# Attention outputs computed token-major and turned afterwards, some by DMA, with filler matmuls at the start and a new plan

## The chip, the cores and the metric

The kernel runs on one core of a Trainium2 chip. The metric is the device time of one execution in microseconds, the median of several executions; the kernel before takes 190.69 us (six runs, 190.32 to 191.94).

## The reference

Two stages follow each other. The first is a gated linear attention over 4 batches, 8 heads, 768 positions and 48 values per head: with f = sigmoid(f_logit) the state S of 48x48 is updated at each position t by

```python
state = f[:, :, t, :, None] * state + np.einsum('bhd,bhe->bhde', k[:, :, t], v[:, :, t])
y[:, :, t] = np.einsum('bhd,bhde->bhe', q[:, :, t], state)
```

The second stage takes y as x, 3072 tokens of 384 values, and computes

```python
h = x @ w_in
g = h * np.cos(h)
return (g @ w_out)
```

Everything comes in and goes out in float32 in DRAM.

## The kernel before, in words

**Tiles.** The 3072 tokens are 24 chunks of 128, six to a batch. Chunks 0 to 11 are worked on two at a time ("pairs" 0, 2, 4, 6, 8, 10, the list DUAL): a pair's tokens are loaded so that each partition holds two neighbouring tokens, an even and an odd one, and all the pair's tiles carry an index e for the two. Chunks 12 to 23 are worked on singly. Each chunk, or pair, goes through these steps, in the words that the code uses as names:

- `decay`: exp and ln of the gate on ScalarE (lines 482 and 494), a prefix sum over tokens on TensorE (`cum`, lines 505 to 517), and its exponentials `b` and `bi` on ScalarE (line 522).
- `attend2` for pairs, `attend` for single chunks. q and k are multiplied by b and bi (`qk`, lines 567 and 680). They are turned so that the head dimension lies on partitions: on TensorE against an identity (`tr`, lines 587 and 698) with a copy out of PSUM (`qkt`), or, for chunks 12 to 22 (TURN_QK), by one DMA transpose issued by SyncE (`tq`, line 689). Then come the scores q times k (`sc`, lines 600 and 711), their mask on VectorE (`am`, lines 606 and 714), k times v for the state (`ps`, lines 620 and 724), the state update (`st` on VectorE, `sz` mostly on GpSimd), and the output y.
- The output y is computed feature-major: features on partitions and tokens along the free axis. For that the 384 features are cut into twelve slices of 32, and each matmul loads 32 columns of v or of the state as weights and streams 128 tokens past them (line 653 for pairs, line 744 for single chunks). VectorE or ScalarE copies the result to the bfloat16 tile xT (`xe`).
- `moe` works on units of 128 or 256 tokens: `h` is x times w_in (line 768, groups of 12 matmuls for 256 tokens), `cos` on ScalarE (line 775), `g` the product on VectorE (line 778), `o` is g times w_out (line 790, groups of four matmuls), `ot` the copy out of PSUM, `st_o` the store. In a pair's chunk the rows of the output are the even and the odd tokens in two blocks, so the chunk is stored by two DMAs of 64 rows each, row by second row (line 799); a single chunk is stored by one (line 802).

The weights are loaded in eight slabs (`w00` to `w13`), each through a buffer of the gT pool, and cast to bfloat16 (line 430).

**What sets the order.** Nothing is scheduled by the hardware or by a compiler. `build` records operations with their possible engines and an estimated cost on each, and with priorities from the table PR; `Plan.run` places them one after the other on the engine that could take them first by these estimates, hands out buffers and PSUM banks, and emits all instructions in that order. PIN fixes the engine of single operations by their number. Each engine works its own list strictly in order. SyncE issues all loads, stores and DMA transposes from one list; a transfer there that waits for a buffer holds up all behind it.

Of the kernel before, what the change touches and what calls it, by code (L numbers as in the profile page):

```python
# [116 lines left out]
class Plan:  # L117
# [4 lines left out]
    FORM = 96.0  # L122
    TABLE = 1290.0
# [34 lines left out]
    def run(self):  # L158
        free = {"PE": 0.0, "ACT": 800.0, "DVE": 3500.0, "POOL": 4500.0, "SP": 750.0}
        table, lock, bus, hot, pe_end, form, sent = None, None, 0.0, 0.0, 0.0, "full", []  # L160
        left = {}
# [8 lines left out]
        while len(order) < n:  # L170
# [46 lines left out]
            o.cost = cost  # L217
            if e == "PE":
                hot *= math.exp((pe_end - s) / 2500.0)
                if hot < 0.5:  # L220
                    cost *= 1.9
                hot = 1.0 - (1.0 - hot) * math.exp(-cost / 2500.0)
                pe_end, form = s + cost, o.form[1]
            o.start = s
            free[e] = s + cost
            if o.dma is not None:
                bus = max(s + cost + 700.0, bus) + o.dma
                o.end = bus + 1250.0
# [19 lines left out]
        order.sort(key=lambda o: (o.start, o.seq))  # L248
        self.makespan = max(o.end for o in order)
# [3 lines left out]
def apart(tc, o, base):  # L253
# [13 lines left out]
    if banks and len(others) == len(banks):  # L267
        for b in banks:
# [8 lines left out]
HALVED = [0, 2]  # L277
TURN_QK = range(12, 23)
PR = {
    "at": [1.29, -46.96, -60.77, -65.31, -72.81, -88.9, -62.2, -78.56, -65.41, -84.16, -49.49, 6.81, 12.89,  # L280
          14.83, 48.99, 87.93, 101.11, 142.54, 101.56, 112.3, 125.58, 54.78, 57.75, 54.86],
    "dec": [47.91, 7.43, -56.35, -90.55, -146.08, -64.43],
    "f": [-34.92, 30.83, -12.01, 57.34, 6.81, 46.82, 6.06, 8.26, 16.01, 51.17, 25.08, -28.88, 70.17, 25.27,
          33.52, 29.11, 45.05, 53.82, 30, 41.02, 75.42, 105.25, 101.8, 47.02],
    "h": [18.15, -30.97, -41.55, -0.98, 22.93, -34.89, 0.62, 10.73, 30.17, 30.71, 68.39, 4.86, 95.08],
    "k": [-26.25, -35.58, -7.84, -14.12, 9.23, 20.62, 9.36, 29.64, 15.73, -3.08, 14.9, 28.23, 13.74, 17.17,
          50.2, 52.92, 39.09, 29.41, 58.65, 34.81, 116.3, 77.26, 139.17, 143.04],
    "o": [24.63, -19.31, 41.7, 78.77, 63.07, 110.4, 28.5, 147.24, 133.25, 171.17, 181.78, 182.53, 223.04],
    "tq": [40.18, 24.86, 49.05, 16.89, -14.63, -13.53, -72.99, 30.71, 100.53, 84.21, 40.41, 92.28, 63.29,
          8.72, -34.92, -31.89, -4.13, 9.55, 29.5, 39.68, 64.12, 95.56, 100.49, 121.09],  # L290
    "v": [-13.48, 17.98, -0.36, -1.26, 5.93, -16.14, 10.21, 31.08, 11.8, 9.11, 19.3, 20.54, 41.94, 22.2,
          47.4, 31.46, 38.38, 19.76, 32.92, 47.16, 53.68, 101.87, 117.21, 44.48],
    "w_in": [-6.83, -2.34, 0.21, 1.62],
    "w_out": [4.81, 3.28, 2.34, 8.4],
    "wc": [-90.87, -90.11, -69.83, -52.76, -136.89, -232, -120.5, -196.66],
    "gate": [None, 8, 6, 1, 19, 12],
}
PIN = {1: "POOL", 3: "ACT", 5: "ACT", 9: "DVE", 11: "POOL", 13: "DVE", 34: "POOL", 37: "POOL", 39: "ACT", 43:
       "ACT", 54: "DVE", 55: "DVE", 82: "DVE", 102: "POOL", 103: "POOL", 104: "DVE", 105: "POOL", 107: "DVE",
       111: "DVE", 124: "ACT", 164: "DVE", 165: "POOL", 167: "ACT", 169: "ACT", 182: "DVE", 204: "DVE", 210:  # L300
       "ACT", 222: "DVE", 228: "DVE", 243: "ACT", 244: "ACT", 283: "POOL", 284: "POOL", 286: "DVE", 293: "ACT",
       306: "ACT", 333: "DVE", 346: "POOL", 347: "POOL", 348: "POOL", 349: "POOL", 364: "ACT", 386: "ACT", 415:
       "ACT", 430: "ACT", 451: "DVE", 457: "DVE", 472: "POOL", 481: "ACT", 487: "ACT", 496: "DVE", 517: "DVE",
       523: "ACT", 547: "DVE", 558: "ACT", 579: "DVE", 585: "DVE", 600: "POOL", 608: "DVE", 623: "ACT", 644:
       "DVE", 665: "POOL", 674: "DVE", 680: "ACT", 689: "DVE", 731: "ACT", 740: "DVE", 746: "ACT", 752: "DVE",
       773: "DVE", 779: "ACT"}


def build(nc, cpool, ppool, q, k, v, f_logit, moe_w_in, moe_w_out, out):
# [13 lines left out]

    ident = tl([128, 128], BF16, "ident")
# [56 lines left out]
    stS = slots("st", 2, [128, NP, 2, D], F32)  # L381
    xS = slots("xT", 5, [128, KM, 256])
# [12 lines left out]
    P.banks = base  # L395
    HB = lambda a, d=D: a.rearrange("p (h d) -> p h d", d=d)
# [36 lines left out]
    def load(t, src, b, c, n, prio, nm, flat=lambda a: a):  # L433

        if n not in DUAL:
            P.op(nm + str(n), {"SP": 430.0}, lambda e: nc.sync.dma_start(
                out=HB(t.ap), in_=src[b, :, c * C:(c + 1) * C, :].rearrange("h p d -> p h d")),
                writes=[t], prio=prio, dma=1050.0)
# [116 lines left out]

    E = lambda e: nc.vector if e == "DVE" else nc.gpsimd

    def attend2(b, c, n, ld, bt, bi, prio):
# [6 lines left out]
        for i in range(2):  # L565
# [8 lines left out]
            reads=[vf], writes=[vb], prio=prio)  # L574
        twin = lambda j, p, e: qkv()[:, j, e, 2 * p:2 * p + 2, :].rearrange("p h d -> p (h d)")
        vv = lambda: vb.ap.rearrange("p (e h d) -> p e h d", e=2, d=64)[:, :, :, 0:D]
        rows = [slice(64 * x, 64 * x + 64) for x in range(2)]
        qkts, ams = [], []
        for i in range(2):
            pt, qkt, sc, am = Val(p1S), Val(qktS), Val(scS), Val(amS)  # L580

            def tr(e, i=i, pt=pt):
# [5 lines left out]
            P.op("tr", {"PE": mm(128, 8)}, tr, reads=[parts[0][i], parts[1][i]], writes=[pt], prio=prio)  # L588
            P.op("qkt", {"DVE": dve(1024, 0.52), "ACT": act(1024)}, lambda e, pt=pt, qkt=qkt: cp(
                e, qkt.ap, pt.ap.bitcast(BF16).rearrange("p (a n) -> p a n", n=C)),  # L590
                reads=[pt], writes=[qkt], prio=prio)

            def scores(e, qkt=qkt, sc=sc):
                o = sc.ap.rearrange("p (r a n) -> p r a n", r=2, n=C)
# [302 lines left out]
```

## Time and profile before

One execution was profiled. Its own time is 190.32 us; the span from its first to its last instruction is 188.5 us, so 1.8 us lie outside the span.

| | |
|---|---|
| median of six runs | 190.69 us |
| profiled execution | 190.32 us |
| span | 188.5 us |
| TensorE busy | 178.5 us, 2512 matmuls |
| VectorE busy | 130.5 us |
| ScalarE busy | 125.8 us |
| GpSimd busy | 68.1 us |
| moved by DMA | 33.14 MB, most of it in packets under 512 B |

The busy time of TensorE counts each matmul from its start to its end, and consecutive matmuls overlap, so it tells that the engine is seldom empty, not how fast it goes. How long a group of matmuls holds the engine is read from the start of the group to the start of the next one, as the chain of waits and the timeline show them.

### The profile page before, as it was taken

How to read it: one execution, taken by the hardware profiler on the slowest of the kernel's cores; microseconds unless marked ns; L12 is line 12 of the kernel's file. 1: busy time of each engine (PE TensorE's matmuls, PEld its weight loads, DVE VectorE, ACT ScalarE, POOL GpSimd, SP SyncE). 2: the span in 40 equal slices, each digit the busy share in tenths (PEclk: the TensorE clock that was granted, in tenths of full speed). 3: DMA queues.
4: the chain of work that ended last, by engine and by line, in shares of the span. 5: the costliest groups of instructions: out<-in, count | busy, mean ns of one | idle time of the engine just before them, and what ended most of it. 6: DMA issues, size and time to landing. Idle time of an engine off the chain costs nothing.

```text
span 188.5 us, 5879 instructions
## 1 busy us (share of the span) xinstructions
PE 178.5 (95%) x2512; PEld 132.8 (70%) x2512; DVE 130.5 (69%) x161; ACT 125.8 (67%) x152; POOL 68.1 (36%) x102
## 2 busy tenths in 40 slices
PE   0889999999999999999999999999999999999993
PEld 0567878666678866678976668856686776788663
DVE  5368798849796939965794285999289399366610
ACT  5771878987377897888899658899662460266411
POOL 8417253019411128793174694026842202000000
PEclk9999999999999999999999999999999999999999
DMA  5999999999998969998999999899710901102022
GB/s 151 271 301 352 381 370 255 287 252 260 251 229 199 228 128 183 226 177 159 188 219 162 187 183 180 169 182 183 170 45 0 122 36 39 48 3 83 0 83 83
DMA packets 94121, 33.14 MB, mean 176 GB/s; under 512 B 87312, under 2 KB 92560, under 8 KB 94096
## 3 DMA queue, kind: packets, MB, share of 16 engines
q1 hardware_dynamic: 94096, 32.78, 76.1%
q8 instruction: 19, 0.31, 0.7%
q14 instruction: 6, 0.05, 0.1%
HBM read 25.17 MB, written 4.72 MB: 159 GB/s over the span
## 4 chain that ended last, share of the span: by engine, by line
PE 82%; DVE 5%; SPq 3%; DMA 2%; ACT 2%; issue 2%; POOL 1%; POOLq 0%; DVEq 0%; ACTq 0%
PE ps L768 33%; PE ps L790 30%; PE ps L653 5%; SPq L444 3%; PE ps L744 3%; DVE qk L567 3%; DMA ld<-in_q_dram 2%; PE ps L711 2%; PE ps L600 2%; PE ps L587 2%; ACT bi L522 1%; PE ps L620 1%; PE ps L514 1%; PE ps L724 1%; ACT b L522 1%
## 5 line engine op out<-in xcount | busy, mean ns | idle before, releaser
L778 DVE TENSOR_TENSOR gT<-ps,cosh 128x1024 bf16<-128x1024 f32 x48 | 58.3, 1221 | 17.2 <-ACT cosh L775 15.3
L775 ACT ACTIVATE cosh<-ps,halfpi 128x1024 bf16<-128x1024 f32 x48 | 53.3, 1114 | 24.8 <-PE ps L768 24.2
L790 PE MATMUL ps<-w_out_bf,gT 128*128 128x384 bf16 (+2 forms) x400 | 69.0, 320 | 0.0
L768 PE MATMUL ps<-xT,w_in_bf 128*128 128x256 bf16 (+1 forms) x624 | 67.2, 268 | 0.0
L768 PEld LDWEIGHTS <-w_in_bf 128*128 128x128 bf16 x624 | 57.6, 100 | 7.8 <-issue 0.2
L790 PEld LDWEIGHTS <-gT 128*128 128x128 bf16 x400 | 36.0, 98 | 21.4
L547 POOL TENSOR_TENSOR sz<-st,b 64x192 bf16<-64x192 f32 x32 | 16.9, 529 | 39.8 <-DVE st L540 38.3
L458 DVE COPY ot<-ps 128x384 f32<-128x384 f32 x14 | 7.6, 552 | 13.0 <-PE ps L790 12.9
L680 POOL TENSOR_TENSOR qk<-ld,b 128x384 bf16<-128x384 f32 x12 | 12.0, 997 | 10.7 <-DMA ld<-in_q_dram 4.9
L606 DVE TENSOR_TENSOR am<-ps,pmask 128x1024 bf16<-128x1024 f32 x12 | 14.3, 1218 | 1.6 <-PE ps L600 1.4
L714 DVE TENSOR_TENSOR am<-ps,umask 128x1024 bf16<-128x1024 f32 x12 | 14.3, 1215 | 0.4 <-PE ps L711 0.4
L540 DVE TENSOR_TENSOR st<-ps,sz 128x384 f32<-128x384 f32 x16 | 8.8, 550 | 7.3 <-PE ps L724 5.9
L458 ACT COPY ot<-ps 128x384 f32<-128x384 f32 (+2 forms) x11 | 5.0, 454 | 13.1 <-PE ps L790 11.9
L430 POOL CAST vb<-ld 128x384 bf16<-128x384 f32 (+1 forms) x11 | 6.8, 621 | 16.1 <-DMA ld<-in_v_dram 8.3
L522 ACT ACTIVATE b<-ps 128x776 f32<-128x776 f32 (+1 forms) x14 | 10.1, 723 | 2.9 <-PE ps L511 2.2
L680 POOL TENSOR_TENSOR qk<-ld,bi 128x384 bf16<-128x384 f32 x12 | 12.0, 999 | 0.1
L482 ACT ACTIVATE f<-f 128x768 f32<-128x768 f32 (+1 forms) x14 | 10.4, 744 | 2.1 <-DMA f<-in_f_logit_dram 2.0
L458 ACT CAST xT<-ps 128x384 bf16<-128x384 f32 x13 | 6.0, 483 | 8.6 <-PE ps L744 6.7
L567 POOL TENSOR_TENSOR qk<-ld,b 128x384 bf16<-128x384 f32 x5 | 6.0, 1197 | 15.6 <-ACT b L522 15.6
L494 ACT ACTIVATE sp<-f 128x768 bf16<-128x768 f32 (+1 forms) x14 | 10.5, 752 | 0.4
L522 ACT ACTIVATE bi<-ps 128x768 f32<-128x768 f32 (+1 forms) x14 | 10.0, 717 | 0.0
L567 POOL TENSOR_TENSOR qk<-ld,bi 128x384 bf16<-128x384 f32 x7 | 7.9, 1135 | 5.1 <-ACT bi L522 5.0
(67 smaller groups left out, 175.7 us busy)
## 6 DMA issues: line engine op xcount, KB each, us to landing
f<-in_f_logit_dram SPq DMA_DIRECT2D x16, 192.0 KB, 3.9
ld<-in_k_dram SPq DMA_DIRECT2D x16, 192.0 KB, 3.9
ld<-in_q_dram SPq DMA_DIRECT2D x16, 192.0 KB, 3.9
gT<-in_moe_w_in_dram SPq DMA_DIRECT2D x4, 768.0 KB, 9.7
gT<-in_moe_w_out_dram SPq DMA_DIRECT2D x4, 768.0 KB, 11.6
ld<-in_v_dram SPq DMA_DIRECT2D x6, 384.0 KB, 5.6
out_dram<-ot SPq DMA_DIRECT2D x24, 96.0 KB, 2.7
ld<-in_v_dram SPq DMA_DIRECT2D x12, 192.0 KB, 3.9
```

Source lines behind the costliest of these rows:

```text
L458: (nc.scalar.copy if e == "ACT" else nc.vector.tensor_copy)(out=o, in_=i_)
L494: nc.scalar.activation(out=o, in_=i_, func=AF.Ln, bias=1.0)
L522: nc.scalar.activation(out=out_.ap[:, s, :], in_=pc.ap.rearrange("p (m n) -> p m n", m=w)[:, :, 0:n], func=AF.Exp, scale=sign)
L547: eng().tensor_mul(out=like(S_out.ap, pv())[s, ..., r, :], in0=srcap()[s, ..., r, :], in1=d[..., None].broadcast_to(list(d.shape) + [D]))
L567: P.op("qk", {"POOL": 1150.0, "DVE": 800.0}, lambda e, j=j, i=i, src=src, dec=dec: E(e).tensor_mul(out=parts[j][i].ap.rearrange("p e h d - ...
L606: P.op("am", {"DVE": dve(1024)}, lambda e, sc=sc, am=am: nc.vector.tensor_mul(out=am.ap.rearrange("p r a n -> p (r a n)").rearrange("p (a ...
L680: P.op("qk", {"POOL": 1020.0}, lambda e, j=j, src=src, dec=dec: E(e).tensor_mul(out=qkv()[:, j, :, 0:D], in0=HB(src.ap), in1=HB(dec.ap[:, ...
L714: P.op("am", {"DVE": dve(1024)}, lambda e: nc.vector.tensor_mul(out=am.ap.rearrange("p r a n -> p (r a) n"), in0=sc.ap.rearrange("p (a n) ...
L768: nc.tensor.matmul(ph.ap[:, g * T:(g + 1) * T], lhsT=w_in_bf[:, f0 // 512, m, f0 % 512:f0 % 512 + 128], rhs=x[:, m, :], start=(g % (G // 2 ...
L775: nc.scalar.activation(out=co.ap, in_=ph.ap, func=AF.Sin, bias=halfpi),
L778: P.op("g", {"DVE": dve(1024)}, lambda e, ph=ph, co=co, gv=gv: nc.vector.tensor_mul(out=gv.ap, in0=ph.ap.rearrange("p (g t) -> p g t", t=T ...
L790: nc.tensor.matmul(po.ap[:, 0:z - a], lhsT=gT.ap[:, j, i * C:(i + 1) * C], rhs=w_out_bf[:, j, a:z], start=(j == 0), stop=(j == KF - 1))
```

## The change

**Output token-major.** Except for pair 0 (the list COLUMNS), y is computed with tokens on partitions: the turned q (128 tokens wide) is the weight and 96 columns of the state stream past it, then the masked scores are the weight and the 48 columns of one head of v stream past. A pair takes 8 + 32 matmuls (4 + 32 without an incoming state) instead of 24 + 64; a single chunk takes 4 + 8 instead of 12 + 16. The new function `finish` then copies y to a bfloat16 tile `yb`, and turns it to feature-major: chunks 14 to 22 (TURN_Y) by a DMA transpose on SyncE's list (`ty`), the others by three transposes on TensorE (`trx`) and a copy out of PSUM (`xe`).

**One store a chunk.** For pairs' chunks the product g is written with the even and odd tokens interleaved again, so that the output rows come in token order; the chunk is stored by one DMA of 128 rows.

**Zeros.** A tile of zeros is filled at the start. Where the plan sees TensorE idle for more than 0.3 us in the early part, matmuls of the zero tile with itself are put into TensorE's list, into a free PSUM bank.

**The plan.** PR and PIN have new values and some cost estimates differ, so nearly every engine's list is in a new order. In the built program TensorE has 107 matmuls of zeros in nine groups (32, 8, 21, 10, 11, 4, 8, 10 and 3), all before the second pair's scores; 39 `trx` transposes; and 2251 matmuls in all. SyncE has 9 `ty` transposes more and 12 stores fewer. VectorE casts three of the four w_in slabs instead of one. The part of the diff that makes pairs turn their q and k by DMA has no effect, since no pair is in TURN_QK.

The functions of the diff, cut to its core:

```diff
+    WARM = 1300.0, 22000.0, 36000.0
...
+            if e == "PE" and self.WARM[0] < s < self.WARM[2] and s - max(pe_end, self.WARM[0]) > 300.0:
+                t0 = max(pe_end, self.WARM[0])
...
+                    warm.append((o, t0, s - 150.0 - t0, min(idle)[1]))
...
+COLUMNS = [0]
+TURN_Y = range(14, 23)
...
+    def keep_warm(t, length, bank):
+
+        w = base["width"]
+        for _ in range(int((length + (320.0 if t < 3000.0 else 0.0)) / (106.0 if t < 3000.0 else 57.0))):
+            nc.tensor.matmul(base["tiles"][bank // 2][:, bank % 2 * w:bank % 2 * w + 128], lhsT=zeros,
+                             rhs=zeros, start=True, stop=True)
...
+    def finish(n, y, ycut, prio):
+
+        yb, x = Val(ybS), xT[n]
+        P.op("yb", {"ACT": act(384), "DVE": dve(384)}, lambda e: cp(e, yb.ap, ycut()),
+             reads=[y], writes=[yb], prio=prio)
+        if n in TURN_Y:
+            P.op("ty", {"SP": 420.0}, lambda e: nc.sync.dma_start_transpose(out=x.ap, in_=yb.ap),
+                 reads=[yb], writes=[x], prio=PR["ty"][n], dma=800.0)
+            return
...
+        def trx(e):
+            for m in range(KM):
+                nc.tensor.transpose(out=pxv()[:, m, :], in_=yb.ap[:, m * 128:(m + 1) * 128], identity=ident)
...
+        P.op("xe", {"DVE": dve(384, 0.52), "ACT": act(384)}, lambda e: cp(e, x.ap, pxv()),
+             reads=[px], writes=[x], prio=prio)
...
+        if n not in COLUMNS:
+            py = Val(scS)
...
+                            nc.tensor.matmul(o, lhsT=qkts[p // 2].ap[:, 2 * x + p % 2, :], rhs=s, start=(p == 0),
+                                             stop=False)
...
+                            nc.tensor.matmul(py.ap[:, o:o + D],
+                                             lhsT=ams[h // 4].ap[rows[x], h % 2, h % 4 // 2 * 2 + t, :],
+                                             rhs=vv()[rows[x], t, h, :],
+                                             start=(S[x] is None and h == 0 and t == 0), stop=(h == H - 1 and t == 1))
...
+        if n not in COLUMNS:
+            py = Val(p1S)
...
+                for h in range(H):
+                    nc.tensor.matmul(py.ap[:, h * D:(h + 1) * D], lhsT=am.ap[:, h % 2, h // 2, :],
+                                     rhs=vb.ap[:, h * 64:h * 64 + D],
+                                     start=(S_in is None and h == 0), stop=(h == H - 1))
...
+            finish(n, py, lambda: py.ap[:, 0:d_model], prio)
...
+                if n0 // 2 * 2 in DUAL:
+
+                    o = o.rearrange("p g (x n e) -> p g x e n", n=64, e=2)
+                    i0, i1 = (v.rearrange("p g (x e n) -> p g x e n", n=64, e=2) for v in (i0, i1))
+                nc.vector.tensor_mul(out=o, in0=i0, in1=i1)
...
-                    if r0 // C // 2 * 2 in DUAL:
-                        for x in range(2):
-                            nc.sync.dma_start(out=out[r0:r0 + C, :].rearrange("(p e) d -> e p d", e=2)[x],
-                                              in_=half.ap[64 * x:64 * x + 64])
-                    else:
-                        nc.sync.dma_start(out=out[r0:r0 + C, a:z], in_=half.ap)
+                    nc.sync.dma_start(out=out[r0:r0 + C, a:z], in_=half.ap)
...
+            if o in P.warm:
+                P.keep_warm(*P.warm[o])
```

## The prediction

> **What bounds the kernel now.** I read the page's rows by slice first, to see which resource is full and when.
>
> ```profile
> PE   0889999999999999999999999999999999999993
> ...
> PEclk9999999999999999999999999999999999999999
> DMA  5999999999998969998999999899710901102022
> ```
>
> TensorE has work from the second slice (each is 4.7 us) to the last. The DMA engines are as full down to the digits 7 and 1 (about 135 us) and nearly empty after them. So there are two candidates: TensorE's list, and, up to 135 us, the order in which loads arrive. Which one waits for the other is read from the chain that ended last.
>
> ```profile
> 13.04 1.15 PE ps L653 x30
> ...
> 18.17 1.24 PE ps L600 x28
> 19.41 2.68 PE ps L768 x24
> 22.09 0.75 PE ps L620 x15
> ...
> 48.46 0.65 PE ps L790 x4
> 49.11 0.78 PE ps L653 x44
> 49.89 0.76 PE ps L790 x4
> ...
> 92.66 0.17 PE ps L724 x4
> ...
> 99.32 0.50 PE ps L744 x28
> ```
>
> From 24 us on this chain is TensorE all but for pieces of 0.2 to 2 us; the idle pieces of TensorE after 26 us add up to 0.8 us. So from there a microsecond less in TensorE's list is a microsecond off the end, as long as its inputs keep up. Before 24 us it is different. The timeline of TensorE shows one group of 24 matmuls of 128 columns twice, at two speeds:
>
> ```profile
> 16.05 1.89 PE L587 MATMUL ps<-ident,qk 128*128 128x128 bf16 x16
> ...
> 19.34 2.74 PE L768 MATMUL ps<-xT,w_in_bf 128*128 128x128 bf16 x24
> ...
> 22.75 1.51 PE L768 MATMUL ps<-xT,w_in_bf 128*128 128x128 bf16 x24
> ```
>
> 112 ns a matmul, then 60. The row of the granted clock shows full speed throughout, so this is another gate. It opens 3.4 us after dense 128x128 matmuls begin at 19.34; the 8 us before, nearly gapless but of small tiles and transposes, did not open it.
>
> **Part 1, y token-major.** Pairs before: 44 matmuls take 0.78 (line 653, 49.11), twice that for a pair, 1.55 without the changes of tile shape. Such a change shows as the 0.76 against 0.65 of the same four matmuls of line 790: 0.11. Pairs 2, 4, 8, 10 have one or two entries (together six, 0.66), pair 6 has no first state (76 x 17.7 ns = 1.33, one entry): 4 x 1.55 + 0.66 + 1.44 = 8.3. After: 8 matmuls of 96 columns at 42 ns (0.17 for four, line 724) are 0.34, one change of shape 0.11, and 32 matmuls of 64 rows and 48 columns, which no row shows. Bounds: 14 ns (line 653, 32 in 0.45) and 28 ns (line 620, the same weight shape with 96 columns, 16 in 0.45). I take 24, nearer to the row with the same weights: 0.77. A pair is 1.22, pair 6 1.05, together 5.9. To it come ten times three transposes of 128 columns at 56 ns (line 587 when warm: 16 in 0.90), 0.17 a chunk, 1.7. Sum 7.6, a gain of 0.7; with 14 ns 2.3, with 28 ns nothing.
>
> Single chunks before: 0.50 with a state (line 744), 0.33 for the two without, plus about ten entries of 0.11: 10 x 0.50 + 0.66 + 1.1 = 6.8. After, all full-shaped, no entry: 4 x 42 + 8 x 27 ns (line 517's one-column matmuls, four in 0.11, are the nearest full-weight row) = 0.39, twice 0.22: 4.3; chunks 12, 13 and 23 add 0.5 for `trx`. Sum 4.9, a gain of 1.9. TensorE's list from 24 us on gets 2.6 us shorter, on the path.
>
> `yb` takes the place of the old copy at the same size (551 ns on VectorE, 483 on ScalarE). The second copy `xe` is new for 13 chunks: between 0.25 (line 458's 678 ns for 1024 columns of bfloat16, by its share) and 0.55; I take 0.4, 8 on VectorE, 5 on ScalarE, some 5 us over both, covered by engines that are 69% and 67% busy. Not covered is the order: `trx` stands in TensorE's list, mostly one group of 0.65 us behind its y, while `yb` needs 0.5 and a hand-over. If `yb` queues behind a 1.1 us cos, TensorE stands. Last of these is chunk 20: between its y and the first `h` that reads it stand 0.65 + 0.17 + 0.65 + 4 x 0.655 = 4.1 us, and `yb` plus a transpose (3.4 us to landing for the larger `tq`) need 4.0. I put 0.8 us of new stalls for all, 0 to 2.
>
> **Part 2, DMA.** What one transpose costs the 16 DMA engines is read from a stretch with two `tq` and one store alone (the last columns are the DMA share and GB/s):
>
> ```profile
> 145.50:148.40 2.90, 2.90 (x60) 1.90 (x49) 1.63 (x4) 0.48 (x1) 1.00 (x2) 1.00 0.57 106
> 148.40:150.00 1.60, 1.60 (x17) 1.42 (x16) 0.00 (x0) 0.88 (x1) 0.00 (x0) 1.00 1.72 124
> ```
>
> 0.57 x 2.9 + 1.72 x 1.6 = 4.4 us, less 0.6 for the store (10 us from 160 us on: share 0.12 at 43 GB/s, two stores), so 1.9 us for 262 KB, and by size 0.72 for a `ty` of 98 KB. The Trainium skill ("DMA: Bandwidth & Descriptors", Latency and other measured facts) gives 261 GB/s for a DMA transpose[...]; that would be 0.38 us. By the page nine `ty` are 3.4 us, by this trace 6.5; the trace decides. On SyncE a `tq` holds the issue for 1.28 us (median of line 689); nine more are 11.5 us, against 12 stores saved at 0.6, 7. SyncE's list has loads in flight for 3.9 us, so 4 us more of issue spread over 50 us are covered; behind a `ty` that waits for its `yb` stand `tq` and loads.
>
> The point where it bites: in the changed order the load of q for chunk 23 stands behind two more `tq`, six `ty` and two more stores: 3.8 + 4.3 + 1.2 = 9.3 us. Before, that load landed at about 132.5 (GpSimd's products resume at 132.88), so now at 138 to 142, by whether the idle 4.5 us of the DMA before 135 (the lower digits of its row) are used. But chunk 23's transposes also stand later: behind them come 24 groups of `h` at 0.655, `o` of eight chunks at 2.6 and 3.6 for the attention of chunks 20 to 23, in all 40.1 us; before it was 51.5. TensorE ended at 185.7; ending at 183 now, it wants them at 143, so the load at 141.5. It just makes it. The same holds near 65 us for q of pair 8, which now stands behind some ten single loads. So a larger gain on TensorE than this is cut off by DMA.
>
> One store a chunk saves DMA issues off the path: 0. The permuted write of 24 `g` has no row. Nothing excludes a loss: at most another 1.22 each, 29 us of VectorE; I take 0, since the operation reads two float32 tiles and its 1221 ns is already 1.2 ns a value. The Trainium skill ("SBUF — State Buffer", Door 1) speaks of 16-byte lines of which two hits are wanted; a step of 4 bytes gives four. No run here shows it.
>
> **Part 3, start.** If the gate were open from 6 us, the chain's cold pieces (1.15 for line 653, 0.85 for a `cum`, then 1.24, 2.68 and 0.75, in all 6.7 us) would shrink by 3.3. By the skill ("TensorE: Matmul & The Clock Gate", What's actually happening) a window of 3.4 us runs freely, so zeros from 1.1 us on open it between 4.5 and 7.9; the trace's 3.4 us from 19.34 to 22.75 fits. Against it: the second group of eight zeros stands ahead of the second `cum` and is counted at 57 ns; still cold it is 0.9 us long and delays that by 0.6. And VectorE has no gap but one from 11.4 to 22 us, and gets two more casts of 0.95 us, while ScalarE loses its two. By hand through the lists: the first pair's second mask ends at 12.7 instead of 14.2; then a cast (0.95), `st` (0.55), and on GpSimd two `sz` (1.05) and a product (1.0) bring the second pair's last product to 16.7, where it was 17.1; transposes 0.45, copy 1.0 (ScalarE), scores 0.35 and the second mask 1.2 end at 20.5 instead of 21.2. The second slab of w_in lands at 19 to 20 as before, behind the same bytes, and its cast on GpSimd (1.5 to 1.8) ends at 21 to 22. From there VectorE has two `st`, two casts, two `g`, a `yb` and two `xe` (6.8 us, and some 0.8 waiting for cos) before unit 2's first `h` at some 28.1, which with eight groups of 0.655 ends at 33.3 instead of 34.1. I take 0.8; the ends are 3.3 and a loss of 0.7.
>
> **Sum.** Against the profiled execution: 188.5 - 2.6 - 0.8 + 0.8 = 185.9 span, 187.7 with the 1.8 around it; the median lies 0.4 above the profiled one, so 188.1.
>
> **Rivals.** (a) The start pays in full and stalls stay out: 190.7 - 2.6 - 3.3 + 0.3 = 185.1. For it: TensorE was gapless from 16 us on though cold; against: VectorE and the slabs of w_in, above. (b) The change doesn't do what it says at the start, or its gain returns as waits: the zeros delay (loss 0.7), `trx` and `xe` wait in VectorE's full stretches (2 us): 190.7 - 2.6 + 0.7 + 2 = 190.8. (c) Slower: a `ty` costs the DMA engines as much as a `tq`, 1.9 us, if a transpose is paid by the row and not by the byte. Then q of chunk 23 lands 6 x 1.2 = 7.1 later, at 149 from the upper end, its products (1.1) and transposes at 150, and 150 + 40.1 + 2.8 of tail + 1.8 + 0.4 = 195.1. It decides against the change from a landing at 144.5, that is from 1.15 us a `ty`. Against it is only the scaling by size. (d) The permuted `g` is slow on VectorE: beyond 0.2 us each, in stretches where it is full, 193 or more.
>
> **Chances.** The forecast 0.45 (its own range 186.3 to 189.9), (a) 0.20, (b) 0.18, (c) 0.13, (d) 0.04. About 0.5% (1 us) is what a measurement of this kernel tells from none. Faster than 189.7: 0.43 + 0.20 + 0.04 = 0.67; within: 0.02 + 0.11 = 0.13; slower: the rest, 0.20. The range 184.6 to 192.0 holds (a) but for its edge, the forecast, (b), and the mild part of (c).
>
> **What would show it.** Line 879's first matmuls at 56 ns and before 17 us: the gate; at 107 ns: not. Line 836 x8 with line 832 x4 in 0.39 and line 718 x32 in 0.77 in the chain. Line 895's mean at 1.22 us: (d) is out. DMA share in a stretch with `ty` alone, and GpSimd's last products (line 774) waiting for q: (c). Waits of TensorE for `yb`: the stalls. The prediction is wrong if TensorE's idle time after 28 us goes beyond 2 us, or if the first `o` does not begin before 34 us.

## The result

The changed kernel takes 189.10 us (median of 29 runs, 187.82 to 190.85) against 191.04 us for the kernel before in the same sessions (66 runs); the ratio is 0.9905, with a 95% interval of 0.9885 to 0.9924. It is 1.9 us faster. The ratio leaves slow executions out, so it is not exactly the quotient of the medians. Forecast were 188.1 us, 2.6 us less than before; the direction and the range held, a quarter of the gain is missing.

The profiled execution of the changed kernel is its slowest (190.85 us, span 189.0), so the lines that follow show one bad start and an ordinary rest. Two more executions of the same kernel were profiled later: the second here took 188.66 us (span 186.9), near the median, the third 191.00 us (span 189.2), the slowest of its group. The rows by slice of the first:

```profile
PE   7997499999999999999999999999999999999993
...
PEclk9999858999999999999999999999999999999999
DMA  5998999899989999967998789969686112210022
```

The zeros fill TensorE's first slices, which were 0 and 8 before. A 4 in the fifth slice (19 to 24 us) was a 9, and after it the granted clock falls. The timeline of TensorE there (start, length, line, tiles, count, and the wait before it):

```profile
5.76 0.33 PE L537 MATMUL ps<-sp,incl 128*128 128x384 bf16 x1
...
15.72 1.50 PE L879 MATMUL ps<-xT,w_in_bf 128*128 128x128 bf16 x24
...
21.33 0.51 PE L686 MATMUL ps<-vb,qk 64*128 64x96 bf16 x16 [0.71 <-DVE am L673]
23.43 2.74 PE L879 MATMUL ps<-xT,w_in_bf 128*128 128x128 bf16 x24 [1.59 <-POOL w_in_bf L462]
...
37.01 1.30 PE L905 MATMUL ps<-w_out_bf,gT 128*128 128x384 bf16 x7
```

The gate is what holds TensorE's matmuls to half speed at first: it is open at 5.76 us (0.33 for a `cum` that took 0.48 at 4.50), and the first `h` runs warm at 15.72, where the kernel before began it cold at 19.34. Then TensorE waits 1.59 us for the second slab of w_in, the gate is closed again (a clock of 0.50 from 22.5 to 29.3 us), the same 24 matmuls take 2.74 instead of 1.50, and the first product with w_out begins at 37.01 us. In the kernel before it began at 34.13:

```profile
34.13 5.36 PE L790 MATMUL ps<-w_out_bf,gT 128*128 128x384 bf16 x32
```

The second profile has no wait for that slab over 0.3 us and an open gate:

```profile
21.58 1.51 PE L879 MATMUL ps<-xT,w_in_bf 128*128 128x128 bf16 x24 [0.26 <-POOL w_in_bf L462]
...
24.16 0.33 PE L710 MATMUL ps<-sz,qkt 128*128 128x96 bf16 x4 [0.90 <-POOL sz L579]
...
34.50 3.73 PE L905 MATMUL ps<-w_out_bf,gT 128*128 128x384 bf16 x22
```

The first `o` is the point at which the time divides, since all of TensorE's list ahead of it is the start (pairs 0 and 2 and the `h` of chunks 0 to 3) in every one of these kernels:

| profiled execution | span | first `o` starts | from there to TensorE's end | of it idle |
|---|---|---|---|---|
| before | 188.5 | 34.13 | 151.5 | 0.8 |
| changed, first profile | 189.0 | 37.01 | 148.8 | 0.9 |
| changed, second profile | 186.9 | 34.50 | 149.2 | 1.3 |
| changed, third profile | 189.2 | 35.15 | 150.8 | 2.4 |

The start gained nothing: it lost 0.4 and 1.0 us where the gate stayed open and 2.9 where it closed. From there on TensorE's work is shorter by 2.8, 2.8 and 2.3 us, and its idle time is longer by 0.2, 0.5 and 1.6, so the rest gained 2.7, 2.3 and 0.7. In the first and the third profile TensorE even ends 0.2 and 0.3 us later than in that of the kernel before, an execution of 190.32 us that is faster than its median. The gain of 1.9 us is thus one of the medians; the profiles show its parts.

What makes the third profile slow, with the gate open throughout, stands among its waits of TensorE, behind the first `o` (total, times, longest):

```profile
PE ps L905 <- DVE w_out_bf L462: 1.4, 1, 1.4
```

TensorE stands for the last slab of w_out, to 42.76 us. It landed at 41.72 us here, at 40.03 and 39.97 in the other two, where the waits are none and 0.30, and at 37.80 in the kernel before, where TensorE did not wait for it.

The new groups stand in the chain that ended last (start, length, line, count):

```profile
52.53 0.36 PE ps L710 x8
52.90 0.50 PE ps L718 x32
...
82.64 0.17 PE ps L602 x3
...
100.23 0.17 PE ps L832 x4
100.40 0.20 PE ps L836 x8
```

A pair's y is 0.86 where it was 1.55, a single chunk's 0.37 where it was 0.50, and three transposes, which are new, take 0.17.

### The profile page after: what moved, and what is told of

It reads as the page before. It is cut to its first block, busy times and chain, and to the rows that moved or that the text cites. A ratio compares the mean times of both kernels' runs of the same rounds, so it can differ in the third digit from the quotient of the medians.

```text
span 189.0 us, 5347 instructions
## 1 busy us (share of the span) xinstructions
PE 179.5 (95%) x2250; PEld 138.4 (73%) x2250; DVE 133.1 (70%) x171; ACT 125.2 (66%) x156; POOL 67.9 (36%) x102
## 4 chain that ended last, share of the span: by engine, by line
PE 75%; SPq 7%; ACT 6%; DMA 4%; DVE 2%; POOL 2%; issue 2%; ACTq 0%
PE ps L879 31%; PE ps L905 30%; SPq L476 6%; DMA gT<-in_moe_w_in_dram 4%; ACT cosh L886 2%; DVE gT L895 2%; PE ps L805 2%; PE ps L653 2%; POOL qk L618 1%; PE ps L718 1%; PE ps L668 1%; PE ps L546 1%; PE ps L836 1%; PE ps L710 1%; PE ps L818 1%
## 5 line engine op out<-in xcount | busy, mean ns | idle before, releaser
L879 PE MATMUL ps<-xT,w_in_bf 128*128 128x256 bf16 (+1 forms) x624 | 70.2, 270 | 2.2 <-POOL w_in_bf L462 1.6
L895 DVE TENSOR_TENSOR gT<-ps,cosh 128x1024 bf16<-128x1024 f32 x48 | 59.7, 1262 | 12.4 <-ACT cosh L886 11.3
L905 PE MATMUL ps<-w_out_bf,gT 128*128 128x384 bf16 (+2 forms) x400 | 67.9, 320 | 0.0
L905 PEld LDWEIGHTS <-gT 128*128 128x128 bf16 x400 | 36.8, 98 | 20.8
L774 POOL TENSOR_TENSOR qk<-ld,b 128x384 bf16<-128x384 f32 x12 | 12.0, 999 | 16.3 <-DMA ld<-in_q_dram 12.2
L618 POOL TENSOR_TENSOR qk<-ld,bi 128x384 bf16<-128x384 f32 x6 | 6.4, 1071 | 21.1 <-ACT bi L554 11.3
L774 POOL TENSOR_TENSOR qk<-ld,bi 128x384 bf16<-128x384 f32 x12 | 12.0, 999 | 0.0
L462 POOL CAST vb<-ld 128x384 bf16<-128x384 f32 (+1 forms) x10 | 6.3, 641 | 15.7 <-DMA ld<-in_v_dram 7.6
L425 PE MATMUL ps<-zeros 128*128 128x128 bf16 x107 | 9.2, 249 | 1.0 <-DVE halfpi L353 1.0
L490 ACT COPY qkt<-ps 128x1024 bf16<-128x1024 bf16 x5 | 5.1, 1014 | 6.2 <-PE ps L653 5.8
## 6 DMA issues: line engine op xcount, KB each, us to landing
out_dram<-ot SPq DMA_DIRECT2D x23, 192.0 KB, 2.2
f<-in_f_logit_dram SPq DMA_DIRECT2D x16, 192.0 KB, 3.7
ld<-in_k_dram SPq DMA_DIRECT2D x16, 192.0 KB, 3.8
ld<-in_q_dram SPq DMA_DIRECT2D x16, 192.0 KB, 3.6
ld<-in_v_dram SPq DMA_DIRECT2D x12, 192.0 KB, 4.2
```

What stands on the lines that cost most here:

```text
L490: (nc.scalar.copy if e == "ACT" else nc.vector.tensor_copy)(out=o, in_=i_)
L774: P.op("qk", {"POOL": 1020.0}, lambda e, j=j, src=src, dec=dec: E(e).tensor_mul(out=qkv()[:, j, :, 0:D], in0=HB(src.ap), in1=HB(dec.ap[:, ...
L879: nc.tensor.matmul(ph.ap[:, g * T:(g + 1) * T], lhsT=w_in_bf[:, f0 // 512, m, f0 % 512:f0 % 512 + 128], rhs=x[:, m, :], start=(g % (G // 2 ...
L895: nc.vector.tensor_mul(out=o, in0=i0, in1=i1)
L905: nc.tensor.matmul(po.ap[:, 0:z - a], lhsT=gT.ap[:, j, i * C:(i + 1) * C], rhs=w_out_bf[:, j, a:z], start=(j == 0), stop=(j == KF - 1))
```

## The experiments

Four kernels shared a chip each time, with the kernel before among them. The changed kernel stands in two of the three groups as it is. On the second chip it did not run; there it is put at 0.9905 of the kernel before, 189.4 us. Its medians elsewhere, 188.9 to 189.1, would make the differences on that chip 0.2 to 0.5 us larger. The kernel before scattered widely (190.8 to 198.1 us on the first chip, 189.4 to 194.0 on the third), so the ratios carry that scatter; differences are taken between the medians of one chip.

| kernel | median us | ratio to before, 95% interval |
|---|---|---|
| first chip: changed kernel | 189.13 | 0.9831 (0.9784 to 0.9878) |
| without zeros | 190.99 | 0.9911 (0.9885 to 0.9936) |
| second slab earlier | 189.24 | 0.9854 (0.9800 to 0.9908) |
| gap filled with zeros | 190.09 | 0.9887 (0.9836 to 0.9939) |
| second chip: before with zeros | 191.34 | 1.0012 (0.9970 to 1.0054) |
| second pair feature-major | 190.17 | 0.9954 (0.9930 to 0.9978) |
| every output feature-major | 195.00 | 1.0213 (1.0171 to 1.0255) |
| outputs turned by TensorE | 193.20 | 1.0127 (1.0089 to 1.0164) |
| third chip: changed kernel | 188.89 | 0.9824 (0.9772 to 0.9877) |
| plain products, two stores | 191.54 | 1.0015 (0.9974 to 1.0057) |
| loads as before | 188.76 | 0.9823 (0.9761 to 0.9886) |
| loads as before, no zeros | 189.01 | 0.9830 (0.9772 to 0.9887) |

### The start: what closes the gate, and what the zeros do

The theory after the first profile was that the wait for the second slab of w_in closes the gate and so eats the gain at the start; the rival, that the zeros themselves delay real work. The changed kernel once more:

> The changed kernel once more, on the chip of the next three. Theory A: TensorE stands for the second slab of w_in at 21.8 to 23.4 us, its gate closes for one or two windows of 3.4 us, and how many is chance; so times spread from 188.0 to 190.5 with a mean clock of 1.00 to 0.98, the median near 189.1. Theory B (the lost time at the start is the zeros themselves, which stand ahead of real work) expects the same median and no tie of time to clock.

189.13 us. Its profile is the third of the section on the result: the gate stayed open although TensorE waited 1.42 us for the slab, and the first `o` began at 35.15. This execution was the slowest of seven, 191.00 us at a mean clock of 0.998, against 188.65 to 189.37 for the others, four of them at 0.99; so time is not tied to the clock alone. Without the zeros:

```diff
-            if o in P.warm:
+            if o in P.warm and False:
```

> The changed kernel in its own order with none of the 107 matmuls of zeros. Theory A: the gate stays shut until some 3.4 us after the dense groups of h begin, everything before costs twice, 1 to 2.5 us slower than the changed kernel: 190 to 191.5. Theory B: real work starts earlier, 0.5 to 1.5 us faster: 187.6 to 188.6.

190.99 us, 1.9 more. So the zeros earn something in this order, which speaks against the rival. In the profile the gate is open by 17.0, the first `h` begins there, 0.8 to 1.3 us later than with zeros, and the first `o` at 35.49. Then the slab's load was put ahead of the load of v for the second pair:

```diff
+        slab = next(o for o in order if o.name == "w01")
+        order.remove(slab)
+        order.insert(next(i for i, o in enumerate(order) if o.name == "v2"), slab)
```

> The changed kernel with one load moved on SyncE: the second slab of w_in ahead of v of the second pair. Theory A: 393 KB less ahead of it at some 330 GB/s, so it lands 1.2 us earlier, h starts 1.2 us earlier and the gate closes less often: 187.3 to 188.3. Theory B: 189.1, as the zeros are the same. A third way: v comes 2 us later and holds up k times v, which stands before h on TensorE; then no gain or a loss of 0.5.

189.24 us, the control's time. The wait for the slab was gone and two others came in its place:

```profile
21.68 0.52 PE L686 MATMUL ps<-vb,qk 64*128 64x96 bf16 x16 [1.23 <-ACT vb L462]
...
24.75 0.33 PE L710 MATMUL ps<-sz,qkt 128*128 128x96 bf16 x4 [0.93 <-POOL sz L579]
...
34.97 3.25 PE L905 MATMUL ps<-w_out_bf,gT 128*128 128x384 bf16 x19
```

v now lands late, which was the third way of the expectation, and the state `sz` comes after it; the first `o` is 0.2 us earlier. The fourth kernel fills the gap with 24 more zeros:

```diff
+        seen = [o for o in order if o.eng == "PE" and o.name in ("ps", "h")]
+        late = seen[[o.name for o in seen].index("ps", 1) + 1]
...
-            if o in P.warm:
-                P.keep_warm(*P.warm[o])
-                bank = P.warm[o][2]
+            if o in P.warm or o is late:
+                fill = P.warm.get(o, (9000.0, 24 * 57.0 + 1.0, 1))
+                P.keep_warm(*fill)
+                bank = fill[2]
```

> The changed kernel with 24 more matmuls of zeros (1.4 us when the gate is open) in front of the h that waits for the second slab; nothing else moves. Theory A: the gate stays open in nearly every run, mean clock 1.000, spread under 1 us, median 188.2 to 188.6. Theory B: more zeros are no help, 189.1 or later. If the gate needs more than this share of dense work to stay open: clock and time as without.

190.09 us, 1 us more than the control's median, with six executions from 189.1 to 191.2 that overlap the control's. In its profile the zeros did not hold the gate (the next lines of the same view):

```profile
21.70 2.68 PE L425 MATMUL ps<-zeros 128*128 128x128 bf16 x24
24.17 2.00 PE L879 MATMUL ps<-xT,w_in_bf 128*128 128x128 bf16 x24
```

At 112 ns each they ran cold themselves, and the `h` behind them began at 24.17 instead of 23.20. So in this execution the gate was lost by 21.7, before the wait, behind a stretch of small groups and waits; in the first profile of the changed kernel TensorE was busy for 2.10 of the 4.20 us from 17.6 to 21.8. And in the control a wait of 1.42 us did not close it. The wait for the slab as the sole cause falls. The half-busy stretch ahead of it does not decide alone either: of these 4.20 us TensorE was busy for 2.62 and 2.40 in the two profiles of the changed kernel that kept the gate open, but for 2.45 here, where it closed, and for 1.87 with the slab earlier, where it stayed open. What decides is open.

The next theory was that TensorE's clock does not set the start at all, but the loads and the elementwise work behind them. Zeros in the kernel before, in its own order:

```diff
+FILL = {0: 32, 1: 8, 2: 14, 3: 8, 4: 10, 7: 8, 10: 8, 11: 10, 13: 6}
...
+            if o in P.warm:
+                P.keep_warm(*P.warm[o])
```

> The kernel before, in its own order, with 104 products of zeros put ahead of nine early TensorE operations, 32 of them ahead of the first. Theory A (TensorE's closed gate sets the start, so that opening it early pays): 0.8 to 2 us faster than before, ratio 0.990 to 0.996, and in the profile the first product with w_out starts at 32.5 to 33.4 us instead of 34.1. Theory C (the start is set by the loads and by the elementwise work behind them, the gated state of the second pair coming at about 24.7 us in every kernel, whatever TensorE's clock): ratio 0.997 to 1.002, h of chunk 0 two to three us earlier, the second pair's y still waiting for its state until about 24.5 us, and the first product with w_out at 33.8 to 34.3 us.

Ratio 1.0012: nothing gained. The profile, of an execution of 193.80 us where the median is 191.34, is less simple than that. The second pair's state came at 23.3 and its y was done at 24.7, 1.4 us earlier than before, against the theory; then, in the middle of a group of `h`, TensorE stood still:

```profile
24.70 0.51 PE L790 MATMUL ps<-xT,w_in_bf 128*128 128x128 bf16 x6
27.45 9.43 PE L790 MATMUL ps<-xT,w_in_bf 128*128 128x128 bf16 x90 [2.24 <-issue]
```

"Issue" is a stop for which the trace shows no releaser; six of twelve matmuls of one operation had run, with the same inputs. So in this execution an early gate did bring the state earlier, and a stop took it back. That the fastest executions with zeros (190.71) are no faster than those without (190.19) says that more than such stops is in it; what, is open.

The last pair of kernels at the start gives the changed kernel the load order of before: k and q of the second pair ahead of the first slab, both slabs ahead of v, the casts on the engines that had them, the first `h` behind the second pair's scores. The rest of the order, the engines and the buffers are those of the changed kernel (with 134 zeros instead of 107), written out as a list and replayed (the first number of each pair is the operation, the second the one it is put behind):

```diff
+MOVED = [(0, 99), (2, 0), (1, 103), (105, 1), (3, 107), (56, 112), (70, 56)]
```

> The kernel after in its own order, but at the start the loads and casts stand as in the kernel before: k and q of the second pair ahead of the first slab of w_in, the second slab ahead of v of that pair, its cast on ScalarE, the first slab's cast on GpSimd, and the first h behind the second pair's scores. Theory L (the order of the loads at the start gives back what the open gate gains there): the second pair's scores start 1 to 1.5 us earlier, its state comes at 23.2 to 23.8 us instead of 24.6, the first product with w_out at 33.6 to 34.3 instead of 35.1 us, and the time is 0.7 to 1.3 us below the control. Rival (the start is bound by the bytes that must land by then, whatever their order): within 0.4 us of the control.

188.76 us, 0.13 below the control and inside the noise: the rival. Its profile has a 1.51 us stop of the "issue" kind ahead of the first `h`, at 19.4, and the first `o` at 35.57, where 33.6 to 34.3 was expected. The same without zeros:

> The same kernel as the one with the loads as before, but with no products of zeros, so that its start is that of the kernel before with token-major outputs and TensorE's gate opens at 16 to 23 us. Theory L: 0.7 to 1.5 us slower than with zeros, which makes it about the control's time. Rival (with the loads in this order the elementwise engines and the loads hide TensorE's slow start, as the kernel before with zeros, at a ratio of 1.001, suggests): within 0.4 us of the kernel with zeros.

189.01 us: no zeros, no early gate, and the control's time; the first `o` begins at 34.65 and TensorE ends 148.8 us later. So with the loads in this order the zeros are worth 0.25 us, inside the noise, and in the changed kernel's own order 1.9. There, two groups of `h` on the first slab stand ahead of the second pair's transposes, so a cold TensorE is late with them: with zeros these `h` begin at 15.7 to 16.2, without at 17.0. Against the second profile, the one without zeros (an execution of 190.39 us) loses 1.0 us at the first `o` and 0.6 behind it; against the third it loses 0.3 at the first `o` and ends 0.6 earlier. So the profiles do not account for all of the 1.9. The same time is reached without zeros, so the early gate is a need of the new order rather than the source of the gain.

What bounds the start in the second profile of the changed kernel is shown by its chain:

```profile
17.75 1.01 ACT qkt L490
18.76 0.74 ACT vb L462
...
19.54 0.63 DVE am L673
...
20.67 0.72 DVE am L673
...
21.80 0.56 DVE st L572
...
22.43 0.51 POOL sz L579
...
23.00 1.12 POOL sz L579
...
27.70 1.12 ACT cosh L886
...
29.02 4.13 SPq L476
...
33.27 6.70 DMA gT<-in_moe_w_out_dram
```

From the second pair's transposes to its state the chain is elementwise work on three engines. The state lands at 24.2 us here and at 25.3 in the same order without zeros; in the order of before it lands at 24.7, and at 23.3 with zeros. So an early gate did bring it 1.1 and 1.4 us forward in these profiles. But the chain goes on, and from 27.7 to 41.0 us TensorE is not in it: behind a `cos`, the load of v holds SyncE's list for 4.1 us, only then is the last slab of w_out issued, it lands at 39.97, is cast on VectorE, and TensorE goes on at 41.01, after a wait of 0.30. It is the slab for which the third profile waits 1.4 us. An earlier first `o` is given back there when the slab is late. No run moved this load, so what its place in SyncE's list costs is not shown.

### The token-major outputs

The second pair alone was put back to feature-major outputs, in the replayed order:

```diff
-COLUMNS = [0]
+COLUMNS = [0, 2]
```

> The kernel after in its own order, engines and buffers, but the pair of chunks 2 and 3 has its outputs column-major as in the kernel before (2 of the 24 chunks). Theory C (the token-major output of this one pair sits on the path at the start: y, copy, three transposes, copy, and only then the wide h): although its y costs 0.7 us more of TensorE, the first product with w_out comes 0.8 to 1.2 us earlier than in the kernel after with an open gate (34.0 to 34.4 us instead of 35.15), and the time is 0.4 to 1 us below after's. Rival (TensorE's list is all that counts): 0.7 to 1.2 us slower than after.

190.17 us, a ratio of 0.9954, so 0.8 above the changed kernel as it is put here: the rival held. Its profile has the gate closed from 21 to 28 us and the first `o` at 36.70, so it does not show the start that was forecast for it. By the time, the copies and transposes that this pair has to go through before its `h` cost less than the shorter y brings, even at the start. Then all outputs:

```diff
-COLUMNS = [0]
+COLUMNS = range(24)
```

> The kernel after in its own order, engines and buffers, with zeros, permuted products and one store a chunk, but every chunk's output column-major as in the kernel before: no copies to yb, no transposes, no turned outputs by DMA. Theory A (the shorter TensorE list of the token-major outputs is the gain of the change, 2.65 us after the start): 2 to 3.5 us slower than after, about as long as the kernel before less 0 to 1 us (ratio to before 0.994 to 1.003). Rival (the order that was planned anew and the zeros carry the gain): within 0.7 us of after, ratio to before about 0.985.

Ratio 1.0213, 5.6 us above the changed kernel, more than the theory's 2 to 3.5. From the first `o` to TensorE's end are 154.7 us against 149.2 in the control's profile. Idle time takes 2.1 of the 5.5 (3.4 us against 1.3); 3.4 us are a longer list. So the list's size is near the theory's, and the replayed order, made for other lengths, adds the waits.

The nine outputs turned by DMA were turned by TensorE instead:

```diff
-TURN_Y = range(14, 23)
+TURN_Y = []
```

> The kernel after in its own order, engines and buffers, but the outputs of chunks 14 to 22 are turned by TensorE (three transposes and a copy each, as for the other chunks) instead of by DMA. Theory A (a turn by DMA takes 0.17 us a chunk off TensorE and costs nothing else): 9 x 0.17 = 1.5 us slower than after. Rival D (the nine transfers cost on the DMA queues and in late q and k what they save, or the later landing holds h back): 0.3 us slower to 0.7 us faster than after, with fewer waits of h for xT.

193.20 us, a ratio of 1.0127, 3.8 us above the changed kernel where 1.5 was expected. The waits of TensorE say what the count of transposes left out (total, times, longest):

```profile
PE ps L621 <- DVE xT L565: 0.5, 1, 0.5
PE ps L882 <- DVE xT L565: 0.5, 1, 0.5
PE ps L909 <- DVE xT L565: 0.5, 1, 0.5
PE ps L895 <- DVE xT L565: 0.4, 1, 0.4
```

Each transpose also takes a PSUM bank until VectorE or ScalarE has copied it out, and the next scores or sums that want that bank wait. From the first `o` to TensorE's end the idle time is 3.2 us against 1.3 in the second profile of the changed kernel, and the list is 2.3 us longer, of which 27 transposes are 1.5; the other 0.8 is not accounted for. Here too the replayed order had no room for these copies, so 3.8 us is the price of undoing this part alone, not what a plan made for it would pay.

### The permuted products and the single store

The control for this and for the two kernels with the loads as before:

> The kernel after, unchanged, as the control for the three kernels beside it: ratio to before 0.987 to 0.992, as in its two earlier runs. In its profile either the clock gate stays open from 5 us on (first product with w_out at about 35.1 us) or it closes at the wait for the second slab of w_in and the first product with w_out comes at 36.5 to 37 us.

188.89 us, with the gate open in its profile, the second of the section on the result, and the first `o` at 34.50. The ratio of 0.9824 is outside the expected 0.987 to 0.992, since the kernel before was slower on this chip (192.25 us), not the changed one faster. Then the products of chunks 0 to 11 in their own order, and two stores for each of these chunks:

```diff
-                if n0 // 2 * 2 in DUAL:
+                if False:
...
-                    nc.sync.dma_start(out=out[r0:r0 + C, a:z], in_=half.ap)
+                    if r0 // C // 2 * 2 in DUAL:
+                        for x in range(2):
+                            nc.sync.dma_start(out=out[r0:r0 + C, :].rearrange("(p e) d -> e p d", e=2)[x],
+                                              in_=half.ap[64 * x:64 * x + 64])
+                    else:
+                        nc.sync.dma_start(out=out[r0:r0 + C, a:z], in_=half.ap)
```

> The kernel after, but the gate products of chunks 0 to 11 are written in their own order and each of these chunks is stored by two transfers of 64 rows, as before. The prediction's step (the permuted write and the single store are worth nothing, VectorE and SyncE having room): the same as the control within 0.4 us, with VectorE's g of these chunks at 1.22 instead of 1.30 us. Rival (the 0.08 us on each permuted product delays h, or the two-row stores crowd SyncE's queue): the permutation costs or saves 0.5 to 1.5 us.

191.54 us against the control's 188.89: 2.65 us slower, with a ratio of 1.0015 to the kernel before that cannot be told from 1. Two things were undone together, but VectorE's `g` did become shorter, 1218 ns in the mean against 1262 in the control, so the loss is put down to the stores; the two were not undone apart. The profile is of the kernel's slowest execution (193.24 us), so its waits are larger than those of an ordinary one. TensorE's longest wait is new:

```profile
PE ps L805 <- DMA qkt<-qk: 2.9, 3, 1.4
```

TensorE waits for turned q and k of single chunks, that is for `tq`; the control's profile has no such wait. SyncE's list shows why; with two stores a chunk:

```profile
83.11 5.09 SPq L914 DMA_DIRECT2D out_dram<-ot  x6
88.31 1.34 SPq L783 DMA_TRANSPOSE qkt<-qk  x1
```

and in the control at the same place in the list:

```profile
82.30 1.34 SPq L783 DMA_TRANSPOSE qkt<-qk  x1
...
89.43 0.52 SPq L912 DMA_DIRECT2D out_dram<-ot  x1
```

Six half-stores hold SyncE for 5.1 us, and the `tq` behind them is issued at 88.3 instead of 82.3. From there SyncE issues without a pause to 125 us, and every later transpose is 4.8 to 7 us later than in the control. The kernel before also had two stores a chunk. That it lacked the nine `ty` cannot be the whole of the difference: the first `ty` is issued at 108.0, and TensorE's first waits for `tq` end at 96.8 and 104.1, before it. In the order of the changed kernel the room on SyncE is needed; two stores without `ty` in that order were not tried.

## Why the prediction was right, and where not

**TensorE's list: right in sum, by two misses that cancel.** It was put at 2.6 us; from the first `o` on TensorE's work is 2.8, 2.8 and 2.3 us shorter in the three profiles. One term was mis-sized: the 32 matmuls of 64 rows and 48 columns. They take 0.50 us to the start of the next group, 15.6 ns each, where "nearer to the row with the same weights" gave 24. By the trace their starts lie 3 and 22 ns apart in turn, so they start in pairs; the same operation as line 620's, with 96 columns, starts 3 and 40 ns apart: 43 ns for two with 96 columns, 25 for two with 48. That is 0.27 us a pair too little gain, 1.1 for the four pairs behind the first `o`. Against it stands a term that the sum left alone: the 480 matmuls of `h` from there on, counted from start to start, hold TensorE for 53.7 us instead of 52.8. Why is open. A single chunk's y (0.37 against 0.39) and the transposes (0.17, up to 0.27 where the group behind follows late) were right. The close sum is luck in part.

**New stalls: 0.8 expected; 0.2, 0.5 and 1.6 found behind the first `o`.** They are not those that were feared: `trx` did not wait for `yb` by more than 0.1 us. The 1.6 are mostly the wait for the last slab of w_out, a term that the sum did not have. After 28 us TensorE is idle for 1.1, 1.6 and 2.7 us in the three profiles; the prediction's own sign of being wrong, over 2 us, is met by the third.

**Turns by DMA: right, between page and size.** From 153 to 156 us one `ty` is the only transfer (the last columns are the DMA share and GB/s):

```profile
153.00:156.00 3.00, 3.00 (x39) 2.30 (x35) 3.00 (x6) 1.61 (x4) 1.00 (x2) 1.00 0.16 33
```

0.16 x 3.0 is 0.48 us of the 16 engines for 98 KB. The Trainium skill's figure ("DMA: Bandwidth & Descriptors", Latency and other measured facts), which it gives for a transpose with a middle dimension that is not contiguous, gave an estimate of 0.38, the scaling from `tq` 0.72. Rival (c), with 1.9, is out. The load of q for chunk 23 was issued at 138.9 us and GpSimd's product of it began at 142.2, the upper end of the 138 to 142 that was forecast; GpSimd waited 12.2 us for q in all, and no wait of TensorE came of it.

**"One store a chunk saves DMA issues off the path: 0": this step failed.** Undone by itself it costs 2.65 us. The text did count SyncE's issue time, 11.5 us more for nine `ty` against 7 saved by 12 stores, and called the difference covered. It summed the list over 50 us and did not ask what stands right behind the stores: three store pairs in a row, with a `tq` behind them, are the place. The single stores are not shown to be a gain over the kernel before, whose order is another; they keep `tq` on time in the new one.

**The permuted product: right.** 0.08 us more on each of 24 (1.30 instead of 1.22; 1262 ns in the mean of all 48 instead of 1218), on an engine with room. Rival (d) is out.

**The start: this step failed.** A gain of 0.8 us was forecast; 0.4 and 1.0 were lost with an open gate and 2.9 in the profile with a closed one. The step's first half held: the gate opened at 4.0 us in the third profile, by 5.8 in the first and at 6.9 in the second (the spacing of the zeros falls from 107 to 56 ns), where 4.5 to 7.9 was the estimate, and the first `h` was warm before 17 us. It is also the gate that the row of the granted clock shows, not another: once it has been open, its closing reads 0.50 there, with the 107 ns again. What failed is the chain by hand behind it. In the second profile, GpSimd's last product for the second pair ended at 18.2 us where 16.7 was forecast: VectorE's second mask of the first pair ended at 13.3 instead of 12.7, a `sz` of 0.36 that the working does not name stood behind it, and two `sz` on GpSimd took 1.6 instead of 1.05. The second pair's masks ended at 21.9 instead of 20.5, and the first `o` came at 34.5 instead of 33.3. In the first profile the sentence "the second slab of w_in lands at 19 to 20 as before, behind the same bytes" failed too. In SyncE's new order the first slab stands ahead of k and q of the second pair, and the second slab behind v, whose issue SyncE held for 3.38 us:

```profile
10.63 3.38 SPq L476 DMA_DIRECT2D ld<-in_v_dram  x1
14.05 2.36 SPq L456 DMA_DIRECT2D gT<-in_moe_w_in_dram  x3
```

It landed at 21.9 there, at 21.6 in the third profile, at 20.0 in the second, and at 18.9 in the kernel before. GpSimd's last product ended at 18.7 in the first profile, having waited 4.7 us for k. But the experiments also say that the order of these loads is not the whole of it: with them as before the time was the same. And the chain behind the first `o`, to the last slab of w_out at 40 to 42 us, was not in the working at all. By the prediction's own test, the first `o` not before 34 us, it was wrong here.

**The sum.** TensorE's end in the second profile against the one before: +0.4 at the start, -2.8 of work and +0.5 of idle time from the first `o` on give -1.9. The forecast had -0.8, -2.6 and +0.8: too much gain at the start, by 1.2 us, while the list and the stalls came out 0.2 and 0.3 better. In the other two profiles the same sum is +0.2 and +0.3. That the median fell inside the range owes much to its width, 184.6 to 192.0. Of the rivals, (b) has the right mechanism at the start (a gain that returns as waits) and the wrong size for the rest; (a), (c) and (d) are out.

## What to carry to other kernels

An issue queue is a resource with a sum and an order of its own: a transfer that looks free off the path can hold up one behind it that is on the path, so price a saving also by what waits if it is absent. Warming TensorE early is worth something only where its own list, and not a chain of elementwise work or a load, sets the end of that stage; and that end is the last load that the stage waits for, not the first product that starts. A part that is undone alone in an order made for it shows what the order needs, which can be far more than the part gains. And one profile is one execution: three of the same kernel put its losses in three different places.

## What the runs showed of the hardware

- The gate that opened at 4.0 to 6.9 us could close again at 21 to 23 us, and in the same program it did in some executions and not in others; how long TensorE was busy in the stretch before did not tell which (1.87 and 2.62 of 4.20 us with the gate staying open, 2.10 and 2.45 with it closing). Over 30 executions of the changed kernel the mean granted clock falls into steps: median 188.6 us at 1.00 (7 runs), 189.3 at 0.99 (18) and 190.4 at 0.98 (5). The first profile has 0.98 and a clock of 0.50 for 6.8 us, which makes 0.018 of 189 us; so a step is about 3.4 us at half clock. The times overlap: the fastest execution, 187.82 us, stands at 0.99.
- TensorE stopped inside or between groups for 0.4 to 2.2 us with no releaser in the trace in four of the eleven profiles of kernels with zeros (0.42, 0.60, 1.51 and 2.24 us the longest in each), for 0.2 at most in the other seven, and for 0.2 at most in the three of kernels without. The cause is open.
- Matmuls of 64 rows of weights and 48 streamed columns start two at a time, 3 and 22 ns apart in turn, 15.6 ns each with the change to the next group; those of 128 rows follow each other every 25 ns (line 836, eight in 0.20).
- A bfloat16 result written at a step of four bytes cost VectorE 0.08 us on 1.22 us for 1024 values a partition.
